# Where a table load, two scales, two squares and the output stores stand in a fused attention and channel-mix kernel

## The chip, the cores and the metric

The kernel runs on one core of a Trainium2 chip. TensorE (PE, with its weight loads PEld), VectorE (DVE), ScalarE (ACT), GpSimd (POOL) and SyncE (SP) run side by side, each through its own list of instructions in order, and wait for each other by semaphores. DMAs are issued by SP and ACT (the queues q1 and q10 of the profile) and by POOL (q0), and are carried out by sixteen DMA engines that all queues share. The metric is the device time of one execution in microseconds (us), of which the median over several runs is compared.

## The reference

Linear attention over 8 batches of 8 heads, 576 tokens and head size 64, normed per head, and then a channel mix over 512 channels with 1,024 hidden ones. Cut to what matters:

```python
kv = np.einsum('bhsd,bhse->bhde', k, v)
out = np.einsum('bhsd,bhde->bhse', q, kv)
rms = np.sqrt(np.mean(out * out, axis=-1, keepdims=True) + 1e-06)
x = out / rms * g_norm                      # then (B, S, H * D)
...
xk = mu_k * x + (1.0 - mu_k) * x_prev       # x_prev: the token before
xr = mu_r * x + (1.0 - mu_r) * x_prev
k = np.maximum(xk @ w_k, 0.0)
v = k * k @ w_v
r = 1.0 / (1.0 + np.exp(-(xr @ w_r)))
return (r * v).astype(np.float32)
```

The output is float32 of shape 8 x 576 x 512, 9.44 MB.

## The kernel before

**Layout.** A batch's 576 tokens are cut into nine blocks of 64: token `9p + j` stands in block `j` at place `p` (`P = 64`, `G = 9`). Two batches together make 1,152 tokens, nine output tiles of 128: tile `t` holds blocks `2t` and `2t + 1` of the pair. Tiles 0 to 3 belong to the even batch, tiles 5 to 8 to the odd one, and tile 4 has the last block of the one and the first of the other. `k`, `v` and `q` are loaded by POOL with a cast to bf16, one batch ahead (`load_all`, L100); each has a single buffer, so a load is issued once PE has read the batch before.

**Periods.** The loop over `b` runs eight periods. Period `b` mixes batch `b` in three stages of units that PE works through in this order: K (`km`: eight chunks of hidden channels, matmul L377, relu L380 on ACT into `rt`, then a square into `sqk`, L386 on ACT or L388 on DVE), R (`r`: one unit for each output tile, matmul L405, sigmoid L408 on ACT into `sig`) and V (`vv`: two units for each tile, eight matmuls L415 in all, after which `finish` multiplies by `sig`, L432 on DVE, and stores). An even period has four tiles, an odd one five. The first two periods do `km` in parts that fit the order in which the tokens come ready, with twelve K units each; their `rt` is `rt0`.

**The plan.** The attention of the next batches is laid between these units by hand: `put(stage, i, ...)` sets steps behind unit `i` of a stage, and each engine gets its instructions in the order in which the program issues them. The steps that matter here are `kv` (matmul L174, copies L113 on ACT or L115 on DVE), `qt` (transposes L188, two copies for each half, on the two engines named), `u` (matmul L210), `square` (L216, ACT), `reduce` and `newton` (DVE), `mult` (`y`, L253, DVE), `flip` (transposes L268, then `move` on ACT, L258, or on DVE, L260), `wrap` and `diff` (DVE), and `blend`: four `scale` steps (L355 on DVE, L353 on ACT) and two `add` steps (L370, DVE). `blend(a, 0, ...)` gives `xk`, which the next period's `km` reads.

**The places that the change touches.** (1) ACT has two table sets. The first is loaded at the start, the second, with the sigmoid, by `ACT.preload_act_table_set` at L543, in the plan of the first period behind K unit 11, the last of that stage. (2) In the plan of the second period, V 6, `blend(a, 0, ACT)` gives two of the four scales to ACT, ahead of a `qt` with copies on ACT, DVE, ACT, ACT. (3) `ACT_SQ = (5, 6, 7)` names the chunks whose square is held back (`later`) and run on ACT in periods 2 to 6, ahead of what stands behind K 7, R 0 and R 1; the other five chunks are squared on DVE at once. `rt` has six buffers. (4) `finish` (L430) writes a tile of 128 x 512 `out_sb`, which has seven buffers, as two stores of 64 rows, one per block, both on SP but for the last two tiles, where SP and ACT take one half each. The last tile is done in pieces of 384 and 128 columns (`last_vv`).

The tile framework gives the DMAs of SP and ACT eight semaphores in turn: a store is issued when the one eight before it has landed, and a buffer of `out_sb` is written again when its stores have landed.

Of the kernel before, what the change touches and what calls it, by code (L numbers as in the profile page):

```python
# [11 lines left out]
BF16 = mybir.dt.bfloat16  # L12
# [6 lines left out]
def run(steps):  # L19
    for s in steps:  # L20
        s()
# [3 lines left out]
def kernel(  # L25
# [13 lines left out]
    nc = tc.nc  # L39

    B, H, S, HD = q.shape
    C = H * HD
# [3 lines left out]
    G = 9  # L46
    P = S // G
    SH = S // 2
    GX = G * HD
    ACT_SQ = (5, 6, 7)  # L50

    ctx.enter_context(tc.manual_schedule())
    const = ctx.enter_context(tc.tile_pool(name="const", bufs=1))
# [1 line left out]
    work = ctx.enter_context(tc.tile_pool(name="work", bufs=2))  # L55
# [4 lines left out]
    ACT, DVE, POOL = nc.scalar, nc.vector, nc.gpsimd  # L60
# [72 lines left out]
    ALL = (0, 1)  # L133
# [22 lines left out]
    def half(i):  # L156
        return slice(64 * i, 64 * i + 64)
# [230 lines left out]
            eng.tensor_mul(out=sqk[:, fcs, o:o + n], in0=src, in1=src)  # L388

    def km(b, fc):  # L390
        rt = work.tile([128, S], BF16, tag="rt", name="rt", bufs=6)
        for h in range(2):
            km_part(b, (fc,), SH * h, SH * h + SH, rt[:, SH * h:SH * h + SH].unsqueeze(1))
        square_ = lambda eng: km_square(fc, S * (b % 2), rt, eng)
        if fc in ACT_SQ and b < B - 1:
            later[b, fc] = square_
        else:
            square_(DVE)

    sig, hold, later = {}, {}, {}  # L400
# [9 lines left out]
    def vv(b, t, part):  # L410
        if part == 0:
            hold[t] = bank(ps_mm, [128, C], FP32, "ps_v")
        ps = hold[t]
        for fc in range(4 * part, 4 * part + 4):
            nc.tensor.matmul(ps, sqk[:, fc, 128 * t:128 * t + 128], wv_sb[:, fc, :],  # L415
                             start=(fc == 0), stop=(fc == NFC - 1))
        if part and (b, t) not in late:
            finish(b, t, queues=(nc.sync, nc.scalar if (b, t) == (B - 1, 7) else nc.sync))

    def last_vv(b, t, part):  # L420

        c = (slice(0, 384), slice(384, C))[part]
        ps = hold[t] = bank(ps_mm, [128, c.stop - c.start], FP32, "ps_v")
        for fc in range(NFC):
            nc.tensor.matmul(ps, sqk[:, fc, 128 * t:128 * t + 128], wv_sb[:, fc, c], start=(fc == 0), stop=(fc == NFC - 1))
        finish(b, t, c, (nc.sync, nc.scalar))

    late = {(0, t) for t in range(4)}

    def finish(b, t, c=slice(0, C), queues=(nc.sync, nc.sync)):  # L430
        o = work.tile([128, c.stop - c.start], FP32, tag="out", name="out_sb", bufs=7)
        DVE.tensor_mul(out=o, in0=hold[t], in1=sig[t][:, c])  # L432
        for i in range(2):
            bb, j = b - b % 2 + (2 * t + i) // G, (2 * t + i) % G
            queues[i].dma_start(out=out[bb].rearrange("(p j) c -> j p c", j=G)[j, :, c], in_=o[half(i), :])

    PARTS0 = ((4 * P, S), (0, 4 * P))
    PARTS1 = ((6 * P, S), (0, 6 * P))
# [30 lines left out]
    hi, lo = PARTS0  # L469
# [65 lines left out]
    for b in range(B):  # L535
        a, a2 = b + 1, b + 2
        plan = {}

        def put(stage, i, *steps):
            plan.setdefault((stage, i), []).extend(steps)  # L540

        def on(f, *args):
            return lambda: f(*args)  # L543
# [17 lines left out]
        def blend(a, which, eng=DVE):  # L561
            return [on(scale, a, which, 0), on(scale, a, which, 1), on(add, a, which, A),
                    on(scale, a, which, 2, eng), on(scale, a, which, 3, eng), on(add, a, which, Z)]

        def part_square(b, fcs, c0, c1):

            return on(km_square, fcs, S * b + c0, rt0[:, fcs, c0:c1], DVE, c1 - c0)
# [3 lines left out]
        if b == 0:  # L571
            put("K", 0, on(mult_c, "y0", even, *lx), on(mult_c, "y1", odd, *lx), on(diff, 0, every, *lo),
                *[on(fused, 0, 0, hp, *lo) for hp in range(NHP)])
            put("K", 5, *[on(scale, 0, 1, hp) for hp in range(NHP)])
            put("K", 8, on(add, 0, 1, A), on(add, 0, 1, Z), part_square(0, slice(0, 4), *hi),
                part_square(0, slice(4, 8), *hi))
            put("K", 10, on(kv, a, ALL, (DVE, DVE)), part_square(0, slice(0, 4), *lo))
            put("K", 11, on(ACT.preload_act_table_set, "sigmoid_and_others"), part_square(0, slice(4, 8), *lo),
                on(warm_mm, 4), on(qt, a, 0, (DVE, ACT)), on(qt, a, 1, (DVE, ACT)))
            all_u(a, "K", 11)  # L580
            put("R", 0, on(reduce, a, 5, 9, ALL))
            put("R", 1, on(reduce, a, 0, 5, ALL))
            put("R", 3, lambda: run(newton(1)))
            put("V", 0, mults(a)[0])
            put("V", 1, mults(a)[1])
            put("V", 3, on(flip, a, 2, 2, ALL, (ACT, ACT)), on(finish, 0, 0), mults(a)[2], on(wrap, a),
                on(diff, a, every, *hi1), *[on(scale, a, 0, hp, DVE, *hi1) for hp in range(NHP)],
                on(add, a, 0, every, *hi1))
            put("V", 5, on(flip, a, 0, 2, ALL, (ACT, ACT)), on(finish, 0, 1), on(finish, 0, 2))
            put("V", 6, on(flip0, a, (ACT, ACT)))  # L590
            put("V", 7, on(diff, a, every, *lo1), on(finish, 0, 3),
                *[on(scale, a, 0, hp, (DVE, ACT)[hp // 2], *lo1) for hp in (0, 2, 1, 3)],
                on(add, a, 0, A, *lo1), on(add, a, 0, Z, *lo1))
        elif b == 1:
            br = blend(1, 1)
            put("K", 1, on(kv, a, ALL, (ACT, ACT), (ps_at, ps_at)))
            put("K", 3, on(qt, a, 0, (ACT, DVE)), on(qt, a, 1, (DVE, DVE)))
            put("K", 4, *br[:3])
            put("K", 5, *br[3:])
            put("K", 6, part_square(1, slice(0, 8), *hi1))  # L600
            put("K", 7, on(u, a, 2, 2, ALL), on(u, a, 0, 2, ALL), on(u, a, 0, 0, ALL), on(square, a, 2, 2, ALL),
                on(reduce, a, 5, 9, ALL))
            put("K", 8, on(square, a, 0, 2, ALL), part_square(1, slice(0, 2), *lo1))
            put("K", 9, on(square, a, 0, 0, ALL))
            put("K", 10, part_square(1, slice(2, 4), *lo1), on(reduce, a, 0, 5, ALL))
            put("K", 11, part_square(1, slice(4, 6), *lo1), part_square(1, slice(6, 8), *lo1))
            put("R", 1, lambda a=a: run(newton(a)))
            put("R", 4, mults(a)[0])
            put("V", 0, mults(a)[1], mults(a)[2])
            put("V", 4, *flips(a))  # L610
            put("V", 5, on(wrap, a), on(diff, a, every), on(kv, a2, ALL, (ACT, ACT)))
            put("V", 6, *blend(a, 0, ACT), on(qt, a2, 0, (ACT, DVE)), on(qt, a2, 1, (ACT, ACT)))
            all_u(a2, "V", 8)
        elif a < B:
            if b == 2:
                br = blend(2, 1)
                put("K", 0, *br[:3])
                put("K", 1, *br[3:])
                put("K", 2, on(reduce, a, 5, 9, ALL))
                put("K", 3, on(reduce, a, 0, 5, ALL))  # L620
                put("K", 5, lambda a=a: run(newton(a)[:4]))
                put("K", 6, lambda a=a: run(newton(a)[4:]))
                put("K", 7, mults(a)[0])
                put("R", 0, mults(a)[1])
                put("R", 1, mults(a)[2])
                put("V", 1, *flips(a), on(wrap, a), on(diff, a, every))
                put("V", 2, *blend(a, 0)[:3])
                put("V", 3, *blend(a, 0)[3:])
                br = 4
            else:  # L630
                put("K", 2, lambda a=a: run(newton(a)[:4]))
                put("K", 3, lambda a=a: run(newton(a)[4:]))
                put("K", 4, mults(a)[0])
                put("K", 5, mults(a)[1])
                put("K", 6, mults(a)[2])
                put("R", 2, *flips(a))
                put("R", 3, on(wrap, a), on(diff, a, every))
                put("V", 0, *blend(a, 0)[:3])
                put("V", 1, *blend(a, 0)[3:])
                br = 2  # L640
            bl = blend(a, 1, ACT)
            put("V", br, *bl[:2], *bl[3:5])
            if 2 < b < B - 2:
                put("V", br + 1, bl[2])
                put("V", br + 2, bl[5])
        if 1 < b < B - 1:
            for n, (stage, i) in enumerate((("K", 7), ("R", 0), ("R", 1))):
                plan.setdefault((stage, i), []).insert(0, lambda n=n: later.pop((b, ACT_SQ[n]))(ACT))
        if b in (3, B - 1):
            put("K", 0, on(add, b, 1, A))  # L650
            put("K", 1, on(add, b, 1, Z))
# [33 lines left out]
```

## Time and profile before

| what | us |
|---|---|
| median of 3 runs (208.08 to 208.49) | 208.13 |
| the profiled execution | 207.85 |
| its span, first to last instruction | 206.1 |
| first store issued (L435) | 37.9 |
| last matmul done, about | 201.7 |
| last store issued, on ACT | 202.6 |
| granted TensorE clock in the profiled execution | 1.0 |

The costliest groups of each engine, from the profile's list (instructions, busy us, mean ns of one): PE `ps_km` L377 x512, 65.5, 286; PE `ps_v` L415 x280, 64.6, 380; ACT relu L380 x120, 50.9, 429; DVE `out_sb` L432 x37, 24.5, 673; DVE square L388 x42, 20.4, 503; ACT sigmoid L408 x36, 21.2, 610; DVE scale L355 x50, 15.5, 355; ACT scale L353 x16, 10.8, 729; ACT square L386 x15, 10.2, 683.

How to read the lines below. A line of the timeline has start, duration, engine, line, operation, what it writes and reads, its shape and a count, and in square brackets how long the engine was idle before it and what ended that. A small q behind an engine's name is its sequencer. A line of the windows view has a stretch, its length, the busy time of PE, PEld, DVE, ACT and POOL (with counts), the granted TensorE clock, the share of the sixteen DMA engines' time that packets took, and GB/s. Packets of two queues can overlap on one engine, so that a share can exceed 1. Bytes of a load are counted after the cast.

### The profile page before, as it was taken

The page shows a single profiled execution, that of the slowest core. Times are in us where ns is not written, and L with a number is a line of the kernel's source. Part 1 is how long each engine was busy: PE and PEld are TensorE (multiplying, and loading weights), DVE is VectorE, ACT ScalarE, POOL GpSimd, SP SyncE. Part 2 cuts the span into 40 slices and gives each one's busy share as a digit, 9 for nine tenths or more (in the row PEclk, how much of TensorE's full clock was granted, in tenths as well). Part 3 has the DMA queues.
Part 4 walks back from the last instruction along what each step waited for, and adds up shares of the span by engine and source line. Part 5 has one row for each costly group of instructions (what it writes and reads, how often), then busy time and mean ns, then how long its engine had stood idle before and what let it go on. Part 6 is the DMA issues. An engine that isn't in the chain of part 4 may idle for free.

```text
span 206.1 us, 6318 instructions
## 1 busy us (share of the span) xinstructions
PE 194.7 (95%) x2684; PEld 115.5 (56%) x2684; DVE 156.6 (76%) x332; ACT 137.9 (67%) x291; POOL 24.8 (12%) x40
## 2 busy tenths in 40 slices
PE   7878979999999999989999999999999999999991
PEld 2435844485444675547654674567554674476441
DVE  2479949989989499699979695999678794974141
ACT  2378594578717888677987389868986489267400
POOL 7940120040004000400022000400000000000000
PEclk9999999999999999999999999999999999999999
DMA  6999999989927990797009970499004600260054
GB/s 225 208 203 208 207 202 204 215 188 178 178 58 144 203 211 0 114 227 214 0 8 154 254 193 0 68 216 266 6 3 105 156 0 3 47 155 3 3 130 124
DMA packets 21360, 27.22 MB, mean 132 GB/s; under 512 B 1740, under 2 KB 16340, under 8 KB 21332
## 3 DMA queue, kind: packets, MB, share of 16 engines
q0 software_dynamic: 14848, 16.19, 48.3%
q1 hardware_dynamic: 6244, 10.36, 18.0%
q8 instruction: 21, 0.34, 0.6%
q10 hardware_dynamic: 240, 0.26, 0.4%
q14 instruction: 7, 0.06, 0.1%
HBM read 33.56 MB, written 9.44 MB: 209 GB/s over the span
## 4 chain that ended last, share of the span: by engine, by line
PE 73%; DVE 9%; DMA 6%; ACT 6%; issue 1%; POOL 1%; DVEq 0%; SPq 0%; ACTq 0%; POOLq 0%
PE ps_km L377 26%; PE ps_v L415 25%; PE ps_r L405 14%; DMA rt<-in_v_dram 4%; DMA out_dram<-out_sb 3%; PE ps_u L210 2%; PE ps_x L268 2%; PE ps_kv L174 2%; PE ps_qt L188 2%; ACT sq L216 2%; DVE y L253 1%; ACT qT L113 1%; DVE out_sb L432 1%; DVE ss L220 1%; ACT rt L380 1%
## 5 line engine op out<-in xcount | busy, mean ns | idle before, releaser
L380 ACT ACTIVATE rt<-ps_km 128x288 bf16<-128x288 f32 (+3 forms) x120 | 50.9, 429 | 23.5 <-PE ps_km L377 15.9
L377 PE MATMUL ps_km<-xk,wk_sb 128*128 128x288 bf16 (+4 forms) x512 | 65.5, 286 | 1.0 <-DVE out_sb L432 0.8
L415 PE MATMUL ps_v<-wv_sb,sqk 128*128 128x512 bf16 x280 | 64.6, 380 | 0.0
L377 PEld LDWEIGHTS <-wk_sb 128*128 128x128 bf16 x512 | 49.3, 98 | 16.7 <-issue 2.1
L415 PEld LDWEIGHTS <-sqk 128*128 128x128 bf16 x280 | 26.1, 98 | 30.0 <-issue 0.2
L432 DVE TENSOR_TENSOR out_sb<-ps_v,sig 128x512 f32<-128x512 f32 (+2 forms) x37 | 24.5, 673 | 16.4 <-PE ps_v L415 15.7
L405 PE MATMUL ps_r<-wr_sb,xr 128*128 128x512 bf16 x144 | 33.1, 379 | 0.0
L388 DVE TENSOR_TENSOR sqk<-rt 128x576 bf16<-128x576 bf16 (+4 forms) x42 | 20.4, 503 | 4.5 <-ACT rt L380 4.5
L408 ACT ACTIVATE sig<-ps_r 128x512 bf16<-128x512 f32 x36 | 21.2, 610 | 2.9 <-PE ps_r L405 2.9
L405 PEld LDWEIGHTS <-xr 128*128 128x128 bf16 x144 | 13.7, 98 | 15.1 <-issue 0.3
L220 DVE TENSOR_REDUCE ss<-sq 128x16 f32<-128x1024 bf16 (+1 forms) x14 | 18.5, 1346 | 2.5 <-ACT sq L216 2.5
L253 DVE TENSOR_TENSOR y<-ps_u,rs 128x512 bf16<-128x512 f32 (+1 forms) x35 | 19.8, 629 | 0.2
L216 ACT ACTIVATE sq<-ps_u 128x512 bf16<-128x512 f32 (+1 forms) x35 | 16.6, 562 | 4.4 <-PE ps_u L210 4.4
L258 ACT ACTIVATE xT<-ps_x,cols 128x128 bf16<-128x128 bf16 (+2 forms) x24 | 12.9, 621 | 8.7 <-PE ps_x L268 8.7
L100 POOL DMA_DIRECT2D in_k<-in_k_dram x7 | 5.2, 747 | 104.2 <-PE ps_kv L174 104.2
L355 DVE TENSOR_SCALAR m<-dx,cols 128x576 bf16<-128x576 bf16 (+2 forms) x50 | 15.5, 355 | 0.3
L113 ACT COPY qT<-ps_qt 128x576 bf16<-128x576 bf16 x19 | 11.1, 645 | 6.2 <-PE ps_qt L314 6.2
L347 DVE TENSOR_TENSOR dx<-xT 128x2304 bf16<-128x2304 bf16 (+4 forms) x11 | 11.3, 1029 | 4.4 <-ACT xT L258 4.2
L353 ACT ACTIVATE m<-dx,cols 128x576 bf16<-128x576 bf16 (+2 forms) x16 | 10.8, 729 | 5.2 <-DVE dx L347 5.2
L370 DVE TENSOR_TENSOR xr<-m,xT 128x1152 bf16<-128x1152 bf16 x16 | 11.7, 755 | 0.1
L370 DVE TENSOR_TENSOR xk<-m,xT 128x1152 bf16<-128x1152 bf16 (+2 forms) x16 | 11.2, 704 | 0.5
L386 ACT ACTIVATE sqk<-rt 128x576 bf16<-128x576 bf16 x15 | 10.2, 683 | 0.0
(64 smaller groups left out, 131.5 us busy)
## 6 DMA issues: line engine op xcount, KB each, us to landing
out_dram<-out_sb SPq DMA_DIRECT2D x69, 128.0 KB, 3.5
in_k<-in_k_dram POOLq DMA_DIRECT2D x7, 576.0 KB, 7.5
in_v<-in_v_dram POOLq DMA_DIRECT2D x7, 576.0 KB, 10.2
in_q<-in_q_dram POOLq DMA_DIRECT2D x7, 576.0 KB, 14.1
wk_sb<-in_moe_w_k_dram POOLq DMA_DIRECT2D x2, 512.0 KB, 9.2
wv_sb<-in_moe_w_v_dram POOLq DMA_DIRECT2D x2, 512.0 KB, 21.5
sqk<-in_k_dram SPq DMA_DIRECT2D x1, 576.0 KB
q<-in_q_dram POOLq DMA_DIRECT2D x2, 288.0 KB, 6.3
```

Source lines behind the costliest of these rows:

```text
L216: ACT.activation(out=sq[:, rg(t0, n, i) if n else slice(0, 1), span(Ms)], in_=ps, func=AF.Square)
L220: DVE.tensor_reduce(out=ss[:, g0:g1, span(Ms)], in_=sq[:, g0:g1, span(Ms)], op=ALU.add, axis=AX.X)
L253: DVE.tensor_mul(out=y[:, g, cts], in0=ps, in1=rs[:, g, cts].unsqueeze(3).to_broadcast([128, max(n, 1), 2 * len(Ms), HD]))
L355: eng.tensor_scalar(out=out_, in0=in_, scalar1=mu, scalar2=None, op0=ALU.mult)
L370: DVE.tensor_add(out=dst, in0=m[:, hs, c0:c1], in1=x[:, hs, c0:c1])
L377: nc.tensor.matmul(ps[:, n, :], wk_sb[:, cc, 128 * fc:128 * fc + 128], at[b]["xk"][:, cc, c0:c1], start=(cc == 0), stop=(cc == NHP - 1))
L380: eng.activation(out=dst, in_=ps, func=AF.Relu)
L388: eng.tensor_mul(out=sqk[:, fcs, o:o + n], in0=src, in1=src)
L405: nc.tensor.matmul(ps, xr[:, cc, 128 * t:128 * t + 128], wr_sb[:, cc, :], start=(cc == 0), stop=(cc == NHP - 1))
L408: ACT.activation(out=sig[t], in_=ps, func=AF.Sigmoid)
L415: nc.tensor.matmul(ps, sqk[:, fc, 128 * t:128 * t + 128], wv_sb[:, fc, :], start=(fc == 0), stop=(fc == NFC - 1))
L432: DVE.tensor_mul(out=o, in0=hold[t], in1=sig[t][:, c])
```

## The change

It makes four edits. The sigmoid's table is loaded on ACT behind K unit 10 of the first period in place of unit 11, so that it stands ahead of the last relu of that stage. In the second period all four k scales of `blend` run on DVE. In the third period (`b == 2`) chunks 3 and 4 are held back too and all five squares run on ACT, one behind each of K 7 and R 0 to R 3; in the other periods the placing stays as it was, and `rt` has seven buffers. And `finish` issues one store for a tile of 128 rows, with `out` seen as two blocks of 64 rows; tile 4 of a pair, whose halves go to two batches, keeps two stores of 64 rows. The last tile's first piece is stored by SP and its second by ACT.

```diff
-    ACT_SQ = (5, 6, 7)
+    ACT_SQ = {b: range(3 if b == 2 else 5, 8) for b in range(2, B - 1)}
...
-        rt = work.tile([128, S], BF16, tag="rt", name="rt", bufs=6)
+        rt = work.tile([128, S], BF16, tag="rt", name="rt", bufs=7)
...
-        if fc in ACT_SQ and b < B - 1:
+        if fc in ACT_SQ.get(b, ()):
             later[b, fc] = square_
...
-            finish(b, t, queues=(nc.sync, nc.scalar if (b, t) == (B - 1, 7) else nc.sync))
+            finish(b, t)
...
-        finish(b, t, c, (nc.sync, nc.scalar))
+        finish(b, t, c, (nc.sync, nc.scalar)[part])
...
-    def finish(b, t, c=slice(0, C), queues=(nc.sync, nc.sync)):
+    def finish(b, t, c=slice(0, C), queue=nc.sync):
         o = work.tile([128, c.stop - c.start], FP32, tag="out", name="out_sb", bufs=7)
         DVE.tensor_mul(out=o, in0=hold[t], in1=sig[t][:, c])
-        for i in range(2):
-            bb, j = b - b % 2 + (2 * t + i) // G, (2 * t + i) % G
-            queues[i].dma_start(out=out[bb].rearrange("(p j) c -> j p c", j=G)[j, :, c], in_=o[half(i), :])
+        b0, by_block = b - b % 2, out.rearrange("b (p j) c -> b j p c", j=G)
+        if 2 * t + 1 == G:
+            for i in range(2):
+                queue.dma_start(out=by_block[b0 + i, (2 * t + i) % G, :, c], in_=o[half(i), :])
+        else:
+            bb, j = b0 + 2 * t // G, 2 * t % G
+            queue.dma_start(out=by_block[bb, j:j + 2, :, c], in_=o)
...
-            put("K", 10, on(kv, a, ALL, (DVE, DVE)), part_square(0, slice(0, 4), *lo))
-            put("K", 11, on(ACT.preload_act_table_set, "sigmoid_and_others"), part_square(0, slice(4, 8), *lo),
+            put("K", 10, on(kv, a, ALL, (DVE, DVE)), on(ACT.preload_act_table_set, "sigmoid_and_others"),
+                part_square(0, slice(0, 4), *lo))
+            put("K", 11, part_square(0, slice(4, 8), *lo),
                 on(warm_mm, 4), on(qt, a, 0, (DVE, ACT)), on(qt, a, 1, (DVE, ACT)))
...
-            put("V", 6, *blend(a, 0, ACT), on(qt, a2, 0, (ACT, DVE)), on(qt, a2, 1, (ACT, ACT)))
+            put("V", 6, *blend(a, 0), on(qt, a2, 0, (ACT, DVE)), on(qt, a2, 1, (ACT, ACT)))
...
-            for n, (stage, i) in enumerate((("K", 7), ("R", 0), ("R", 1))):
-                plan.setdefault((stage, i), []).insert(0, lambda n=n: later.pop((b, ACT_SQ[n]))(ACT))
+            for n, fc in enumerate(ACT_SQ[b]):
+                plan.setdefault(("R", n - 1) if n else ("K", 7), []).insert(0, lambda fc=fc: later.pop((b, fc))(ACT))
```

As the built program has them, a whole-tile store reads 128 partitions x 512 and writes `out` as 2 x 64 x 512; the last tile's pieces have 384 and 128 in place of 512. Before, each store had 64 x 512 on both sides.

## The prediction

> **What bounds the kernel now.** I read the page's busy times and its chain of waits first.
>
> ```profile
> span 206.1 us, 6318 instructions
> ...
> PE 194.7 (95%) x2684; PEld 115.5 (56%) x2684; DVE 156.6 (76%) x332; ACT 137.9 (67%) x291; POOL 24.8 (12%) x40
> ...
> PE 73%; DVE 9%; DMA 6%; ACT 6%; issue 1%; POOL 1%; DVEq 0%; SPq 0%; ACTq 0%; POOLq 0%
> ```
>
> The chain is PE's own work for 73% of the span; stores appear on it for 2.7%. So today DVE, ACT and the stores matter only where PE waits for them, and three of the four edits are aimed at such places. The fourth touches a resource that has room now, so next I read the DMA queues and issues.
>
> ```profile
> q0 software_dynamic: 14848, 16.19, 48.3%
> q1 hardware_dynamic: 6244, 10.36, 18.0%
> ...
> out_dram<-out_sb SPq DMA_DIRECT2D x69, 128.0 KB, 3.5
> ...
> rows<-in_moe_mu_k_dram SPq DMA_DIRECT2D x1, 2.0 KB
> ```
>
> Columns of the first two: packets, MB, share of 16 engines; of the others: issues, KB each, us to landing. Loads take half of the sixteen engines, stores under a fifth, spread evenly. To price one packet I asked for three windows: stores queued back to back, loads alone, stores that come singly. After the PEclk column stand the DMA share and GB/s.
>
> ```profile
> 95.00:95.50 0.50, 0.50 (x7) 0.40 (x5) 0.50 (x2) 0.41 (x1) 0.00 (x0) 1.00 1.06 366
> 110.00:113.00 3.00, 3.00 (x52) 1.56 (x50) 3.00 (x7) 1.82 (x5) 0.00 (x0) 1.00 1.18 190
> 197.00:198.00 1.00, 1.00 (x6) 0.49 (x5) 0.32 (x1) 0.00 (x0) 0.00 (x0) 1.00 0.87 197
> ```
>
> One engine moves 366/16 = 22.9 GB/s of queued stores, a 2,048 B row in 89.5 ns; 190/16 = 11.9 GB/s of loads, a 1,152 B packet in 97 ns; and single stores at 197/16/0.87 = 14.2 GB/s, 144 ns a row.
>
> **Edit four, the stores (L434-435).** It removes 33 of 74 issues of some 0.5 us from SP and ACT, and changes the shape of what is left: 64 rows on both sides before; now 128 partitions in `out_sb`, but 2 x 64 rows in `out`, the 2 outermost. What decides is over how many engines such a transfer is spread. This trace answers for other shapes. A DMA's semaphore gets sixteen steps; in the trace's semaphore events the four-row `mu_k` load (L92, issued at 1.76 us) has one step at 2.29, 3.4 us ahead of its data, and then four single ones at 5.69 to 5.92; the one-row `g_norm` load has one early and one late; the 64-row store issued at 41.43 has sixteen single ones, 43.57 to 44.27. Four rows run on four engines, one on one, 64 on sixteen. For 2 x 64 against 128 no transfer here answers; the bounds are 2 engines (the outermost count of `out`, as the small loads go) and 16 (the partition count). I take 2: in those loads the outermost count is the engine count, and a split into sixteen would have to cut through the 2 on one side and not on the other.
>
> [...]
>
> Then every whole-tile store puts 64 rows on each of two engines: 64 x 89.5 ns = 5.7 us, against 4 rows on each of sixteen now. Per pair of batches these two carry 8 x 5.7 us of stores and 6 loads x 32 packets x 97 ns = 18.6 us: 64 us of work in about 47 us of span (first stores at 37.9, 84.9, 133.0). They never run empty after the first store, and the end is a sum of their work. Stores: 31 tiles x 64, the last tile's 1,536 B and 512 B pieces worth another 64, and the middle tile's two 64-row stores, four times 8: 2,080 rows x 89.5 ns = 186.2 us. Loads still to come at 38 us: about 17 (two of the third batch, five batches of three) x 32 x 97 ns = 52.8 us. Start: first store's issue 37.9, less 0.6 (edit one below), plus 1.1 from issue to first packet (180.52 to 181.64 in the trace). 38.4 + 186.2 + 52.8 = 277.4; the last packet now ends some 1.9 us before the span does: 279.3. The profiled execution took 207.85 for a span of 206.1, and the median, 208.13, is 0.28 above it: 279.3 + 1.75 + 0.3 = 281.3.
>
> The price of a row is bounded by 84 ns (shortest usual 2,048 B packet in the trace) and 144 (single stores). I take 89.5: with 64 rows behind each other the engine always has the next one, as at 95 us. At 84 the sum is 270; at 144 it is 395.
>
> What waits: `out_sb` has seven buffers, so L432 on DVE waits for the store seven tiles earlier, and SP's next issue for the one eight earlier. Behind L432 on DVE stand the blends (L355, L370), and PE's km (L377) waits for those and for the bank that L432 reads. The loads share the two engines, so `in_q` lands later and PE's transposes (L188) wait. These waits don't add to the sum; they are how PE learns of it. PE would end near 240, and the last seven stores drain alone.
>
> **Edit one, the table load (L543).** ACT's part now:
>
> ```profile
> 25.54 0.60 ACT L380 ACTIVATE rt<-ps_km 128x512 bf16<-128x512 f32 x1 [1.09 <-PE ps_km L377]
> 26.15 1.28 ACT L543 ACT_TABLE_LOAD   x1
> 27.44 1.18 ACT L113 COPY qT<-ps_qt 128x576 bf16<-128x576 bf16 x2
> ```
>
> ACT is idle for 1.09 us ahead of the last relu. The load moves there, from 24.45 to 25.73, and overhangs by 0.2: the relu ends at 26.35, DVE's square (L388) and its qT copies behind it come 0.2 later. ACT's copies start when the transposes are done, 26.82 as DVE's do now, not 27.44. The last u matmuls wait for ACT's second copy, so PE gains 0.6 us. If the gap weren't there, the load would cost 1.28 as now.
>
> **Edit two, the k scales of the second period (V 6).** DVE takes two more scales ahead of its qT copy; ACT gives up 1.44 us.
>
> ```profile
> 66.56 0.45 DVE L115 COPY qT<-ps_qt 128x576 bf16<-128x576 bf16 x1
> ...
> 67.07 0.23 PE L210 MATMUL ps_u<-kv,qT 64*128 64x64 bf16 x4 [0.43 <-DVE qT L115]
> 67.51 0.80 PE L210 MATMUL ps_u<-kv,qT 64*128 64x64 bf16 x34 [0.21 <-ACT qT L113]
> ```
>
> PE waits for both copies here. Two scales are 0.64 us: DVE's copy ends at 67.65 in place of 67.01, ACT's is early, and the last matmuls start some 67.8, not 67.5. A loss of 0.3.
>
> **Edit three, five squares on ACT.** DVE drops two squares of 0.37 us in a stretch (71 to 83 us) that it fills; its y (L253) frees the bank for the transposes at 82.6 by up to 0.45 us earlier. ACT gains two squares, 0.59 us each after overlap, ahead of four sigmoids; 0.96 of it lies in its idle time before `kv`, the rest delays qT and xT, which dx waits for. I take 0.2 gained, between 0 and 0.45. The seventh `rt` costs nothing.
>
> Alone, edits one to three would give 0.5 us; with the stores as above only the 0.6 ahead of the first store counts.
>
> **Rivals.**
> (A) The stores still run on sixteen engines. Then the four edits add up: 0.5, and at the end ACT's piece is issued at 202.2 in place of 202.6, with DMA 85% busy from 202 to 204: 0.3 more. 208.1 - 0.8 = 207.3, faster. For it: the partition count is 128. Against it: the four-row load.
> (B) Two engines, but 144 ns a row throughout: 395. Against: at 95 us queued stores ran at 89.5.
> (C) Two engines, other ones for each transfer. Then only the drain shows: the last store issued at 202, 1.1 to its first packet, 64 rows of 1,536 B at three quarters of 89.5 (4.3), 0.9 to landing, 1.3 to the end: span 209.6 less 0.5; time 211. Against: nothing here shows such a turn; it decides if the engines take turns.
> (D) The gains are given back: 208.1.
>
> **Chances.** Forecast 0.76, own range 268 to 310 (84 ns, and 102 if loads and stores hinder each other); A 0.13, B 0.03, C 0.05, D 0.03. The range has to reach from A, 206.5, over C to the forecast's top, with some room, 318: 0.9 of the weight, because without A and C too much is left out. Measurement can tell 0.2% (0.4 us). Faster: most of A, 0.11. Within: D and the rest of A, 0.04. Slower: 0.85.
>
> **What would show it.** Right: the chain ends in long DMA `out_dram` pieces, landing of a store near 6 to 45 us instead of 3.5, `out_sb` on DVE waiting for DMA, DMA share low (two of sixteen) yet GB/s near 45 at the end, last matmul long before the span's end, and two late semaphore steps per store. Edit one: qT at 26.8 in ACT's line, whatever the stores do. Wrong: a store landing within 4 us, with sixteen steps.

## The result, and the profile after

| | before | changed |
|---|---|---|
| median, us | 208.11 (207.97 to 208.49) | 260.62 (260.55 to 260.75) |
| ratio, 95% interval | | 1.2521 (1.2499 to 1.2542) |
| span of the profiled execution, us | 206.1 | 258.8 |

The changed kernel is slower by a quarter. Its page, in the same order as before: busy times, DMA in 40 slices, the chain of waits.

```profile
span 258.8 us, 6270 instructions
...
PE 199.3 (77%) x2684; PEld 116.8 (45%) x2684; DVE 156.8 (61%) x332; ACT 137.4 (53%) x291; POOL 24.7 (10%) x40
...
PEclk9999999999799999998558999999999999955555
DMA  7999996952961791198122198111311111121110
...
PE 43%; DMA 38%; DVE 4%; ACT 2%; issue 1%; POOL 1%; SPq 0%; DVEq 0%; POOLq 0%
```

PE runs the same 2,684 matmuls as before, but its share of the chain has fallen from 73% to 43%, and DMA's has risen from 6% to 38%. The DMA row explains how: from the middle on most slices show a 1. That is one tenth of sixteen engines, and not a sign of idle DMAs but of two engines that never rest: from 39 to 256 us, no half microsecond of the trace without load packets has a DMA share under 0.12. The windows view (busy time of PE, PEld, DVE, ACT and POOL, then PEclk, DMA share, GB/s) says it to the digit:

```profile
215.00:221.00 6.00, 6.00 (x29) 2.74 (x28) 1.93 (x3) 0.60 (x1) 0.00 (x0) 1.00 0.14 54
240.00:250.00 10.00, 0.00 (x0) 0.00 (x0) 0.00 (x0) 0.00 (x0) 0.00 (x0) 0.50 0.13 51
```

Two of sixteen are 0.125. In the second window every compute engine is done and the stores alone are left: 51 GB/s, 25.5 for each of the two, a row of 2,048 B in 80.3 ns. The semaphore events agree: the whole-tile store issued at 75.17 us has one step at 84.08, just after its issue ends, and two more at 106.53 and 106.98, where a 64-row store of before had sixteen. Late in the run the steps of successive whole-tile stores come 5.13 us apart, 80 ns for each of 64 rows, and the two late steps of every store come within 1.8 us of each other.

The DMA issues (KB each) and, from the view of tile `out_sb`, the issue times in ns (shortest, median, longest):

```profile
out_dram<-out_sb SPq DMA_DIRECT2D x31, 256.0 KB
in_k<-in_k_dram POOLq DMA_DIRECT2D x7, 576.0 KB, 10.3
...
in_q<-in_q_dram POOLq DMA_DIRECT2D x7, 576.0 KB, 20.2
```

```profile
L439 SPq DMA_DIRECT2D out_dram<-out_sb x32: 521/4953/11028, 37.6 to 240.1; - x32
```

No landing time stands behind the stores: the page gives one only where all DMAs of a semaphore show sixteen steps each, and here every one of the eight semaphores has whole-tile stores. By the steps, these land 8.8 to 34.0 us after their issue, 18.9 in the median, against 3.5 before. Loads land later too, 20.2 us in the median for `in_q` against 14.1. That a part of each load waits on the two engines behind stores is argued from this, as the trace doesn't name the engine of a packet. And an issue that took about half a microsecond now holds SP for 4.95 us, which is about what 64 rows at 80 ns take: SP is let go at the pace of the two engines.

How PE learns of it, from PE's and DVE's parts of the timeline:

```profile
65.72 0.83 PE L188 MATMUL ps_qt<-ident,in_q 64*64 64x64 bf16 x72 [2.37 <-DMA in_q<-in_q_dram]
...
123.44 1.12 PE L377 MATMUL ps_km<-xk,wk_sb 128*128 128x288 bf16 x4 [4.48 <-DVE out_sb L432]
133.19 9.42 PE L377 MATMUL ps_km<-xk,wk_sb 128*128 128x288 bf16 x56 [8.64 <-DVE out_sb L432]
184.45 7.02 PE L377 MATMUL ps_km<-xk,wk_sb 128*128 128x288 bf16 x56 [3.11 <-DVE out_sb L432]
```

```profile
122.69 0.69 DVE L432 TENSOR_TENSOR out_sb<-ps_v,sig 128x512 f32<-128x512 f32 x1 [6.85 <-DMA out_dram<-out_sb]
132.45 0.69 DVE L432 TENSOR_TENSOR out_sb<-ps_v,sig 128x512 f32<-128x512 f32 x1 [9.07 <-DMA out_dram<-out_sb]
```

DVE's multiply waits for a store of seven tiles before to free its buffer, and PE's km waits for that multiply. PE's last matmul:

```profile
221.92 1.91 PE L425 MATMUL ps_v<-wv_sb,sqk 128*128 128x384 bf16 x16
```

It ends at 223.8, some 22 us later than before; DVE's last multiply ends at 231.2, and some 26 us of stores follow it. So of the 52.7 us by which the span grew, PE's waits, with the lower clock that follows them, make 22, and the stores that drain behind PE the rest.

### The profile page after: what moved, and what is told of

It reads as the page before. It is cut to its first block, busy times and chain, and to the rows that moved or that the text cites. A ratio compares the mean times of both kernels' runs of the same rounds, so it can differ in the third digit from the quotient of the medians.

```text
span 258.8 us, 6270 instructions
## 1 busy us (share of the span) xinstructions
PE 199.3 (77%) x2684; PEld 116.8 (45%) x2684; DVE 156.8 (61%) x332; ACT 137.4 (53%) x291; POOL 24.7 (10%) x40
## 4 chain that ended last, share of the span: by engine, by line
PE 43%; DMA 38%; DVE 4%; ACT 2%; issue 1%; POOL 1%; SPq 0%; DVEq 0%; POOLq 0%
DMA out_dram<-out_sb 27%; PE ps_km L377 21%; PE ps_v L415 12%; DMA in_q<-in_q_dram 8%; PE ps_r L405 5%; DMA rt<-in_v_dram 3%; DVE out_sb L432 1%; PE ps_u L210 1%; PE ps_x L268 1%; PE ps_qt L188 1%; PE ps_kv L174 1%; DMA in_k<-in_k_dram 1%; ACT rt L380 1%; POOL q L90 1%; DVE m L355 1%
## 5 line engine op out<-in xcount | busy, mean ns | idle before, releaser
L377 PE MATMUL ps_km<-xk,wk_sb 128*128 128x288 bf16 (+4 forms) x512 | 68.9, 294 | 17.2 <-DVE out_sb L432 17.0
L377 PEld LDWEIGHTS <-wk_sb 128*128 128x128 bf16 x512 | 50.4, 100 | 35.2 <-issue 19.0
L415 PE MATMUL ps_v<-wv_sb,sqk 128*128 128x512 bf16 x280 | 66.2, 387 | 0.0
L432 DVE TENSOR_TENSOR out_sb<-ps_v,sig 128x512 f32<-128x512 f32 (+2 forms) x37 | 24.6, 672 | 42.6 <-DMA out_dram<-out_sb 27.8
L388 DVE TENSOR_TENSOR sqk<-rt 128x576 bf16<-128x576 bf16 (+4 forms) x40 | 19.5, 505 | 6.3 <-ACT rt L380 6.3
L253 DVE TENSOR_TENSOR y<-ps_u,rs 128x512 bf16<-128x512 f32 (+1 forms) x35 | 19.8, 628 | 0.2
L355 DVE TENSOR_SCALAR m<-dx,cols 128x576 bf16<-128x576 bf16 (+2 forms) x52 | 16.1, 356 | 0.3
L386 ACT ACTIVATE sqk<-rt 128x576 bf16<-128x576 bf16 x17 | 11.6, 685 | 0.0
L353 ACT ACTIVATE m<-dx,cols 128x576 bf16<-128x576 bf16 (+2 forms) x14 | 9.4, 722 | 3.9 <-DVE dx L347 3.9
## 6 DMA issues: line engine op xcount, KB each, us to landing
in_q<-in_q_dram POOLq DMA_DIRECT2D x7, 576.0 KB, 20.2
```

The source lines that it names most:

```text
L253: DVE.tensor_mul(out=y[:, g, cts], in0=ps, in1=rs[:, g, cts].unsqueeze(3).to_broadcast([128, max(n, 1), 2 * len(Ms), HD]))
L355: eng.tensor_scalar(out=out_, in0=in_, scalar1=mu, scalar2=None, op0=ALU.mult)
L377: nc.tensor.matmul(ps[:, n, :], wk_sb[:, cc, 128 * fc:128 * fc + 128], at[b]["xk"][:, cc, c0:c1], start=(cc == 0), stop=(cc == NHP - 1))
```

## The experiments

### Which edit does it

The store edit alone on the kernel before, and the other three edits without it.

```diff
 stores alone: finish, vv and last_vv as in the change, all else as before
 without stores: ACT_SQ, rt's buffers, table load and blend as in the change, finish as before
```

> The kernel before with the store edit alone. Theory (each whole-tile store runs on two DMA engines, whose work from the first store on sets the end): the other three edits matter only by the 0.6 us that they bring the first store forward, so 261.2 us, between 260.5 and 262. Rival (one of the other edits, such as the squares held back on ScalarE, makes a good part of the 52 us): well below 255.

> The three other edits with the stores of before. Prediction's terms: 0.6 gained by the table, 0.3 lost by the scales, 0.2 gained by the squares, so 0.5 faster than before, 207.6 us. Rival (they hinder each other, or their waits cost more): 208.1 or above.

Measured: 260.68 us with the stores alone (ratio 1.2524, interval 1.2499 to 1.2549), and 207.55 without them (ratio 0.9979, 0.9959 to 0.9999). The whole loss is the store edit's. Whether the other three bring the end forward by the 0.6 us of an earlier first store can't be told: the two kernels with the new stores are 0.06 apart in their medians. In their profiled executions the first store is issued at 38.66 and 37.61, but 0.6 of that is a first km that starts later (17.28 and 16.68).

### Is it the engine count, or the shape and size of the store

Each store of before was cut in two by rows, so that all of them stay plain rows on both sides and small. Only the row counts differ between the two kernels; 62 has no divisor from 3 to 16, 60 has 15.

```diff
-            queues[i].dma_start(out=out[bb].rearrange("(p j) c -> j p c", j=G)[j, :, c], in_=o[half(i), :])
+            rows = out[bb].rearrange("(p j) c -> j p c", j=G)[j, :, c]
+            for lo_, hi_ in ((0, 62), (62, 64)):      # the control: ((0, 60), (60, 64))
+                queues[i].dma_start(out=rows[lo_:hi_], in_=o[64 * i + lo_:64 * i + hi_, :])
```

> The kernel before, each store of 64 rows cut into one of 62 and one of 2 rows, both still plain two-dimensional on both sides. Theory (the engine count is the largest up to 16 that divides the outermost count): 62 gives 2 and 2 gives 2, so each of 36 tiles puts 64 rows on each of two engines. At the 80 ns a row that the changed kernel shows, 2,304 rows in place of 2,080 are 17.9 us more than the changed kernel: 279 us (274 to 284). Rival (the long time comes from the two-block shape of the store itself, or from single stores of 256 KB): 208 to 211.

> The control: 60 and 4 rows in place of 64, as many issues as with 62 and 2. Theory: 60 rows run on 15 engines and 4 on 4, no engine is overloaded, 208 to 210 us (twice the issues cost up to 1 us at the end). Rival (uneven row counts or the number of issues cost the time): the same 270 to 284 as with 62 and 2.

Measured, in one execution of each: 279.27 us with 62 and 2, 210.39 with 60 and 4. Windows of the kernel with 62 and 2 rows, and then of the control (columns as above):

```profile
260.00:270.00 10.00, 0.00 (x0) 0.00 (x0) 0.00 (x0) 0.00 (x0) 0.00 (x0) 0.50 0.13 49
```

```profile
197.00:203.00 6.00, 5.21 (x32) 2.69 (x31) 2.83 (x5) 0.00 (x0) 0.00 (x0) 1.00 0.45 149
```

The first again shows two engines and 49 GB/s, with stores that have the shape of before; the control moves 149 GB/s. So it is neither the 256 KB of a store nor its two blocks: it is the number of engines, and a row count of 62 makes it two just as well. The semaphores say so for every store: one early and two late steps for each of 62 or of 2 rows, sixteen in all for each of 60 rows, one early and four late for each of 4. The 279 was worked out from 80 ns a row and 224 more rows on each engine (2,304 against 2,080), and fell within 0.3 us. The control's 210.39 is 0.4 above its expected range. In its trace PE's last matmul ends 0.53 later than before, as much as this execution's first km starts later, and the last store is issued at 205.71, where before it was 202.57: the rest lies in the queue of issues at the end. The counts of packets tell 62 from 60 as well. ACT's queue q10 has three stores of 64 rows before, with 240 packets: 192 of rows and 48 of 4 B, sixteen for a store. Cut into 62 and 2 rows they have 204, so 4 beside each 64 rows, and into 60 and 4 rows 249, so 19: two and two, fifteen and four, if a 4 B packet stands for an engine. Read so, the engine count in these runs is the largest up to 16 that divides the row count, for 62, 2, 60, 4 and 64 rows.

### From which point it decides

One store for tiles 0 to 3 of each pair only, and then for tiles 5 to 8 only: sixteen tiles with whole stores each, two 64-row stores for the others (minus is the changed kernel).

```diff
-        if 2 * t + 1 == G:
+        if 2 * t + 1 == G or b % 2 == 1:      # the other: b % 2 == 0
...
-                queue.dma_start(out=by_block[b0 + i, (2 * t + i) % G, :, c], in_=o[half(i), :])
+                queue.dma_start(out=by_block[b0 + (2 * t + i) // G, (2 * t + i) % G, :, c], in_=o[half(i), :])
```

> The kernel before, with one store for tiles 0 to 3 of each pair alone (16 of the 32 whole-tile stores). Theory (two engines whose work piles up, and only what is left at the end or late for a load is paid): four stores are 4 x 64 rows x 80 ns = 20.5 us on each of the two engines and six loads 18.6, against 47 us for a pair, so the pile is gone before the next one; the last four, from 178 us, are done by about 200. What is paid is some 3 us of late loads early on: 211 us (208.5 to 214). Rival (each such store costs the same wherever it stands, 52.6 / 32 = 1.64 us): 234.

> The other 16: one store for tiles 5 to 8 of each pair alone. Theory: the pile of a pair is gone too before the next, but the last four stores start at 197.4 us and take 20.5 us: last packet near 219, span near 221, time near 223, and up to 3 more for loads of the fifth batch behind the first pile (221 to 227). Rival (each store costs the same): 234, as with the even periods.

Measured, in one execution of each: 211.08 and 228.06 us, 3.0 and 20.0 above the run of before beside them. Together that is 23, not 52: the price is not one per store. The third period's km in the kernel before, and then PE's transposes in the two kernels, the even periods first:

```profile
92.31 3.94 PE L377 MATMUL ps_km<-xk,wk_sb 128*128 128x288 bf16 x30 [0.76 <-DVE out_sb L432]
```

```profile
65.97 0.83 PE L188 MATMUL ps_qt<-ident,in_q 64*64 64x64 bf16 x72 [2.28 <-DMA in_q<-in_q_dram]
```

```profile
85.44 0.83 PE L188 MATMUL ps_qt<-ident,in_q 64*64 64x64 bf16 x72 [3.04 <-DMA in_q<-in_q_dram]
```

With the even periods the pile is worked off between the pairs, and what is paid is, but for 0.3 us, one late `in_q`: the third period's km, at 92.31 before, resumes at 95.08, and PE's last matmul ends as much later. With the odd ones the same kind of wait puts it at 96.26, some 3.8 us once the 0.16 by which this execution's first km starts later is taken off, and the last four stores, the first of them issued at 201.29, have their last packet at 224.55. That is 1 us beyond the expected range: the late load took 0.8 more than the 3 allowed, and the last pile 1.6 us more than its 256 rows at 80 ns and the start of 1.1. By the semaphores most of the 1.6 lies in the first of the four stores, whose late steps come 7.9 us after its issue, where the 1.1 and its 64 rows make 6.2; why it was slow is not shown. In neither kernel is DVE seen to wait for a store. When all 32 are whole, a pair's work on the two engines (64 us by the prediction, 60 at 80 ns) exceeds its 47 us, the pile of one pair is still there when the next begins, and DVE's buffers run out. The point from which it decides lies between the two: 39 us of work in a pair's 47 leave no pile, 60 do. That it is the 47 itself is worked out, and no run tried a count between.

### The three small edits

Each alone, and the two that were forecast as gains together.

```diff
 table: the load behind K unit 10 in place of 11
 scales: *blend(a, 0, ACT)  ->  *blend(a, 0)   in V 6 of the second period
 squares: five held-back squares in the third period, rt with seven buffers
```

> The table edit alone. Prediction's term: ScalarE's copies of the first period start when the transposes are done and not behind the load, 0.6 us for TensorE: 207.4 us, the last u matmuls of that period 0.6 earlier in the trace. Rival (a load lands late and takes the gain back before the second period): 208.0, with the u matmuls early and the second period's first km not.

> The scales edit alone. Prediction's term: VectorE's qT copy ends 0.64 later and TensorE's u matmuls wait for it, a loss of 0.3 us: 208.3 us, the 34 u matmuls starting near 67.8 and not 67.5. Rival (the freed ScalarE is worth more than the copy costs): 207.8 or below.

> The squares edit alone. Prediction's term: 0.2 us gained (0 to 0.45): 207.8 us, with TensorE's transposes of the third period free 0.3 to 0.45 earlier and ScalarE's kv copies some 0.1 to 0.2 later. Rival (ScalarE's delay reaches dx and eats it): 208.0 or above.

> Table and squares, without scales and stores: the two terms that were forecast as gains. 0.8 us faster than before, 207.2 us, and 0.3 faster than with the scales edit too (207.55 measured). Rival (the scales edit costs nothing or helps): 207.5 or above.

| | us | ratio to before, 95% interval |
|---|---|---|
| table | 207.6 | 0.9975 (0.9964 to 0.9986) |
| scales | 208.42 | 1.0006 (0.9991 to 1.0021) |
| squares | 207.99 | 0.9989 (0.998 to 0.9998) |
| table and squares | 207.35 | 0.9965 (0.9951 to 0.9978) |

Before had 208.15 beside these. Table and squares without the other two has the lowest median of all kernels run. It is clearly below before, but only 0.2 and not 0.3 below the 207.55 with the scales edit too, and the two intervals overlap. The scales' loss lies within its interval and is read from the trace. PE before and then ACT and PE with the table edit, PE with the scales edit, and for the squares edit PE before, then PE and ACT with the edit:

```profile
28.68 0.79 PE L210 MATMUL ps_u<-kv,qT 64*128 64x64 bf16 x34 [0.31 <-ACT qT L113]
```

```profile
25.09 1.28 ACT L543 ACT_TABLE_LOAD   x1
26.38 0.60 ACT L380 ACTIVATE rt<-ps_km 128x512 bf16<-128x512 f32 x1
27.49 1.18 ACT L113 COPY qT<-ps_qt 128x576 bf16<-128x576 bf16 x2 [0.51 <-PE ps_qt L188]
```

```profile
28.13 1.39 PE L210 MATMUL ps_u<-kv,qT 64*128 64x64 bf16 x40 [0.38 <-DVE qT L115]
```

```profile
67.08 0.20 PE L210 MATMUL ps_u<-kv,qT 64*128 64x64 bf16 x2
67.99 0.85 PE L210 MATMUL ps_u<-kv,qT 64*128 64x64 bf16 x38 [0.71 <-DVE qT L115]
```

```profile
81.95 1.11 PE L188 MATMUL ps_qt<-ident,in_q 64*64 64x64 bf16 x72
```

```profile
82.32 0.89 PE L188 MATMUL ps_qt<-ident,in_q 64*64 64x64 bf16 x72
```

```profile
84.79 1.63 ACT L258 ACTIVATE xT<-ps_x,cols 128x1024 bf16<-128x1024 bf16 x3
```

Table: the load now stands ahead of the relu, and the copies wait for the transposes, as forecast. From the relu of K unit 10 (ends 24.45 before, 25.08 here) to the end of the u matmuls it takes 4.44 us and not 5.02: 0.58 gained. Scales: the copy that PE waits for is DVE's, and the wait of 0.43 and 0.21 has become one of 0.71. The third period's km resumes at 92.84 against 92.31, with 0.16 of this execution's later start: 0.37 lost. Squares: the transposes take 0.89 and not 1.11. DVE's `y` (L253) ends at 82.30, ahead of them, where before it ended at 82.55, while they ran; that it is the bank which they waited for is argued from this. But xT on ACT follows its own copies without the idle 0.36 of before; km resumes at 92.45, and with a start 0.26 later than before that is 0.12 gained.

## Why the prediction was right

**The stores.** Its main step, two engines of sixteen for a store whose one side has 2 outermost, holds (a share of 0.13 in the drain, two late steps for a store), and so does what follows: two engines that work from the first store to the end, DVE waiting for buffers, PE for DVE and for late loads, the last stores draining alone. The sixteen steps that it gives to a DMA are what the traces show for the 64-row stores and the loads of the batches; the four-row load has five step events and a whole-tile store three. It came out 20.7 us too long, 281.3 against 260.6, below the 268 that it gave as its own range's lower end. One term was mis-sized: 89.5 ns a row, taken from stores of before that were queued back to back on all sixteen engines at 366 GB/s, and it measured 80.3 where two engines work alone. 2,080 rows x 9.2 ns is 19.1 us. With 80.3 in its place the sum reads 38.4 + 167.0 + 52.8 + 1.9 = 260.1, for a span of 258.8. The 1.3 left over are in the count of loads: in the changed trace the last two of the 17 land at 39.88 and 42.62, so that about half of one was done at 38.4, and 16.5 loads (51.2 us) make the sum 258.5, an estimate.

The price had two faults. The window taken for it was the slowest of the four looked at near 95 us; two of the others, also of the kernel before, read

```profile
94.50:95.00 0.50, 0.50 (x7) 0.40 (x5) 0.50 (x1) 0.41 (x1) 0.00 (x0) 1.00 1.08 374
94.90:95.90 1.00, 1.00 (x11) 0.80 (x9) 1.00 (x3) 0.78 (x3) 0.00 (x0) 1.00 1.08 379
```

which is 87.6 and 86.5 ns a row, so that 2 to 3 of the 9.2 ns were the choice of window. The rest is that two engines alone ran faster each than sixteen together; why is not shown. The lower bound of 84, the shortest usual packet, was no bound: in the drain the packets still take 84 ns, but one follows the other every 80.3, so packets of one engine overlap a little, here those of a single queue (a share of 0.13 is 2.1 engines' time from two).

**What waits.** As named: L432 for the store seven tiles earlier (27.8 us on DVE in all), PE's km behind it (17.0 us), PE's transposes behind `in_q` (2.37 us). PE's end was put near 240 and was 223.8, for the same 9.2 ns: some 1,670 rows were done by then, and 9.2 ns on each are 15 us. The stores' landings, 8.8 to 34.0 us, lie within the 6 to 45 named as a sign.

**The small edits.** 0.6 gained, 0.3 lost and 0.2 gained were forecast; by the traces it is 0.58, 0.37 and 0.12. Together that is 0.33 gained where 0.5 was forecast; by the medians the three gained 0.47, 207.55 us against a forecast of 207.6. In the changed kernel none of it can be told in the time. Its trace has the sign named for edit one: ACT's qT copies start at 27.14, which is 26.86 once the 0.28 by which its first km starts later is taken off.

**The rivals.** A (sixteen engines) falls with the semaphore steps and the windows, B (144 ns throughout) with 80.3, C (other engines each time) with the 0.13 and 0.14 of the windows without loads, and with the 5.13 us between the steps of successive stores, as turns would let waiting stores run side by side. D falls with the time.

**Not tried.** If the two blocks stood interleaved, row by row, in the tile's partitions, `out` would have 64 outermost. That such a whole-tile store would run on sixteen engines is an estimate, from the sixteen steps of the stores of before, which have 64 outermost. No kernel here has it.

## What to carry to other kernels

Before merging DMAs, look at the outermost count on both sides of the merged one, the DRAM side too: fewer, larger transfers can land on fewer engines, here two of sixteen, and a low DMA share on the page (0.13 here) can be a saturated pair. A resource that is far from full as a mean has to be costed per engine, against the time until the work comes again. Where that work fits, only what is left at the end, or what delays a load, is paid: with half of these stores the same edit costs 3 us or 20, by where they stand. Where it doesn't fit, the pile grows and the engines wait for it: with all of them it costs 52. Price a packet from its throughput in a state like the one to come, since neither its own duration (84 ns) nor its rate among sixteen busy engines (89.5) gave the 80.3 measured.

## What the runs showed of the hardware

**The granted clock.** In the first of PE's two longest waits for the stores (4.48 and 8.64 us) its granted clock fell to 0.50, at 121.1, and it stayed there through the second and for some us after it: back to 1.00 at 138.1, 4.9 us after PE resumed at 133.2 (a mean of 0.73 from 136 to 140). In the wait of 3.11 us ahead of 184.45 it stayed at 1.00. In the changed kernel, PEclk ahead of the DMA share and GB/s:

```profile
126.00:133.00 7.00, 0.00 (x0) 0.00 (x0) 0.55 (x1) 0.00 (x0) 0.00 (x0) 0.50 0.14 41
133.20:136.00 2.80, 2.80 (x12) 1.72 (x12) 2.80 (x4) 0.82 (x2) 0.00 (x0) 0.50 0.36 98
136.00:140.00 4.00, 4.00 (x25) 2.79 (x24) 2.28 (x10) 2.33 (x6) 0.00 (x0) 0.73 0.27 80
140.00:144.00 4.00, 4.00 (x30) 2.67 (x28) 3.49 (x8) 3.52 (x9) 0.00 (x0) 1.00 0.13 51
```

The 56 km matmuls behind the wait took 9.42 us, 168 ns each, where 64 take 7.84 (123 ns) at the full clock. That is some 2.5 us lost on PE, and it costs nothing that the runs show, as the two engines have stores waiting all the while and these set the end. The mean granted clock of the profiled execution, 0.90 in place of 1.0, comes from three stretches at 0.50: 66.5 to 69.9, just after PE's wait for `in_q`, 121.1 to 138.1, and from 226.9 on, when PE is done. It is thus read as an effect of the waits and not a cause of the time.

**The issue.** A store that finds its two engines behind holds SP's issue for 4.95 us in the median and 11.0 at most, against 0.59 before. The stores of 64 rows were held as well, 2.8 us in the median. After the first 3.1 us SP issues nothing but stores, so no load stood behind them; what a load on that queue would lose, no run shows.
